# Summing the weight blocks of w_in elsewhere: from attention into slots and units

## The chip, the cores and the metric

The kernel runs on one core of a Trainium2 chip. The metric is the device time of one launch in microseconds, as the median of repeated runs. The core has five engines with queues of their own: TensorE (PE; its weight loads are shown apart as PEld), VectorE (DVE), ScalarE (ACT), GpSimd (POOL) and SyncE (SP), and sixteen DMA engines. GpSimd and SyncE issue most of the DMAs.

## The reference

Three parts follow each other, each fed by the one before:

```python
proj = einsum('bhsd,df->bhsf', x, w_phi)                 # attention, x = q and k
phi  = concat([exp(proj - max|proj|), exp(-(proj - max|proj|))])
kv, z = einsum('bhsf,bhsd->bhfd', k_p, v), sum(k_p, axis=2)
attn = einsum('bhsf,bhfd->bhsd', q_p, kv) / (q_p . z + 1e-6)

expert_idx = argmax(xn @ en.T / tau)                     # MoE, 8 experts, top 1
out[mask] = gate * (relu(x[mask] @ w1[e]) @ w2[e])

h = x @ w_in                                             # dense layer
out = (h * sigmoid(h)) @ w_out
```

Attention has 4 batches of 8 heads, 576 positions, head size 64 and 128 features. The MoE has 2304 tokens of 512 and experts of 1024. The dense layer goes 512 to 2048 to 512. All is fp32, except that w_in and w_out arrive as 64-bit floats.

## The kernel before

**Attention.** A loop `for g in range(-2, G)` runs over the 32 heads (G = 32). In each turn TensorE projects a head, multiplies phi(k) with v and phi(q) with kv, and works on neighbouring heads at the same time. VectorE's part of a head is always the same: the maximum (m, line 390), the difference (d, L391), the copy of kv (L470), the division (rd, lh and x, L486 to L491). GpSimd makes the low parts of fp32 operands (zl, L376; vl, L406; kl, L429). An fp32 matrix is split into a high part that TensorE multiplies at full rate and a low part that is what is left; a product is then three matmuls. Behind the last line of VectorE's work of a head stands, in chosen turns, other work: routing for the MoE (lines 557 to 617) and the preparation of w_in.

**Preparing w_in.** w_in is read as pairs of 32-bit integers and narrowed to fp32 on the chip by a chain of integer instructions (`narrow`, lines 179 to 205, one row of the profile for each step). Ten blocks of it, conversion step k = 0 to 9, are done in attention, in the turns listed in CONV, and more in the slots. The class `Convert` holds their buffers (raw). Two such blocks make a pair. The dense layer multiplies by Strassen-Winograd's scheme with seven products instead of eight, which needs four sums of the pair's four 256-column parts: `sums` makes them by three instructions, one over both of two parts (L174, 128x2x256) and two over one part (L177, 128x256). What comes out, seven columns of 256, is stored in DRAM (sscr, one for each of eight pairs) and fetched again later. Before the change pairs 2 to 6 are summed in attention by VectorE, two pairs by GpSimd in slots 11 and 16 (`csum`), and the last by VectorE in the third unit (`wsum`).

**Slots.** The MoE runs as 22 slots of 128 tokens (three more only run if the routing needs them). In a slot GpSimd gathers the tokens (xg), TensorE multiplies with w1 into ph and, after ScalarE's hh, with w2 into py. VectorE subtracts (xl, hl and the low part of the weights), ScalarE casts the high parts (wh, hh). Weights are loaded into buffers called raw. Between a slot's steps stand the remaining conversion of w_in and w_out and its loads and stores: STEPS gives (slot, step) of each VectorE and ScalarE piece, SLOTWORK those of loads (`cload`), sums (`csum`) and stores (`cstore`). Loads and stores in SLOTWORK are issued by GpSimd, in its own queue, in the order of the code, as are the gathers.

**Units.** The dense layer h = x @ w_in is 32 units: 8 pairs of column blocks for each of 4 groups of tokens, each of seven products (n) of about 0.8 us on TensorE, into puA, puB and puC, which ScalarE copies and VectorE joins (ht, L1120). In the first eight units each pair's weights are fetched from sscr (`wfetch`), copied to the high part (`whigh`, ScalarE) and reduced to the low part (`wlow`, VectorE, L1010, 128x1792). A list `at(u, n, task)` tells behind which product of which unit a task stands:

```python
for q in range(2, NJP):
    at(q - 2, 6, whigh, q)
    at(q - 1, 5, wlow, q)
at(1, 4, wfetch, 6)
at(2, 4, wfetch, 7)
at(3, 1, wsum)
```

The last layer multiplies with w_out and scatters to the output; the change doesn't touch it. All engines take their instructions in the order in which the code writes them; each waits for what its next instruction needs, and what stands behind it waits too.

Of the kernel before, what the change touches and what calls it, by code (L numbers as in the profile page):

```python
# [45 lines left out]
CT = 4  # L46
G = B * H
# [5 lines left out]
SUMS = 27  # L53
# [15 lines left out]
def moe_kernel(ctx, tc, qk, v, w_phi, emb, tau, w1, w2, win, wout, out):  # L69
# [11 lines left out]
    sscr = [dram.tile([P, 7 if i < NJP - 1 else 4, 256], F32, name=f"sscr{i}") for i in range(NJP)]  # L81
# [129 lines left out]
    class Convert:  # L211
# [3 lines left out]
        def region(self, p):  # L215
            return self.a[:, 2048:4096] if p == CA // 2 - 1 else self.b[:, p % 2 * 2048:(p % 2 + 1) * 2048]

        def load(self, i):
            o = (i + 1) % 3 * 1024
            self.h[i] = self.a[:, o:o + 1024].bitcast(I32).rearrange("p (f t) -> p f t", t=2)  # L220
            fetch_raw(i + CT, self.h[i])

        def step(self, k):
            if k + 2 < CA:
                self.load(k + 2)
            if k > 1:
                p = k // 2 - 1
                r = self.region(p).rearrange("p (a f) -> p a f", a=8)
                if k % 2 == 0:
                    self.s[p] = sums(r, nc.vector)  # L230
                    next(self.s[p])
                else:
                    next(self.s.pop(p), None)
            if k < CA:
                o = 512 * (k % 2 == 0)
                c = self.region(k // 2)[:, o:o + 512].bitcast(I32)
                todo = narrow(self.h.pop(k), c, k)
                next(todo)
# [12 lines left out]

    def phase_all(ctx):
# [725 lines left out]
        def wspace(q):  # L978
            if q == NJP - 1:
                W[q] = [wlast(0), None]  # L980
                return
            wb = (big.tile([P, 2, 2048], F32R, tag="blk", name="wb") if q < 4 else
                  pools["ur"].tile([P, 2, 7 * 256], F32R, tag=f"wb{q}", name="wbr", bufs=1))
            W[q] = wb[:, 0, 0:7 * 256], wb[:, 1, 0:7 * 256]

        def wlast(i, dt=F32R):
            return pools["ur"].tile([P, 7 * 256], dt, tag=f"wb{NJP - 1}{i}", name="wbr", bufs=1)

        def wfetch(q):
            if q < NJP - 1:  # L990
                if q not in W:
                    wspace(q)
                nc.sync.dma_start(out=W[q][1].bitcast(F32), in_=sscr[q].rearrange("p a f -> p (a f)"))
            else:
                W["r"] = pools["ul"].tile([P, 2048], F32, tag="ws", name="ws", bufs=2)
                nc.sync.dma_start(out=W["r"][:, 0:1024], in_=sscr[q].rearrange("p a f -> p (a f)"))

        def wsum():
            for _ in sums(W["r"].rearrange("p (a f) -> p a f", a=8), nc.vector):
                pass  # L1000

        def whigh(q):
            src = W[q][1].bitcast(F32) if q < NJP - 1 else W["r"][:, 256:]
            nc.scalar.copy(out=W[q][0], in_=src)

        def wlow(q):
            src = W[q][1].bitcast(F32) if q < NJP - 1 else W["r"][:, 256:]
            if q == NJP - 1:
                W[q][1] = wlast(1)
            nc.vector.tensor_tensor(out=W[q][1], in0=src, in1=W[q][0].bitcast(F32), op=ALU.subtract)  # L1010
# [207 lines left out]
        def rest():  # L1218
            xr = pools["ur"].tile([P, 2, TN], F32, tag="xf2", name="xf2", bufs=2)
            xr = xr.rearrange("p c t -> p (c t)")[:, 0:512]  # L1220
            rw, hs = FR[:, 0:512], FR[:, 512:1536]
            t1 = pools["ul"].tile([P, 2048], F32R, tag="ws", name="fr", bufs=2)
            ch_, cl_, xh_, xl_ = (t1[:, i * 512:(i + 1) * 512] for i in range(4))
# [64 lines left out]
        cv = Convert(*(raw2[i].rearrange("p k f -> p (k f)") for i in (1, 0)))  # L1288
        first = None
# [11 lines left out]
        for g in range(-2, G):  # L1301
# [231 lines left out]
        FR = wlast(1, F32)  # L1533
# [106 lines left out]
```

## Time and profile before

| | us |
|---|---|
| median of three runs (932.51 to 935.31) | 933.13 |
| profiled execution | 939.35 |
| its span in the trace | 937.6 |
| TensorE busy | 908.7 |
| VectorE busy | 643.5 |
| ScalarE busy | 583.0 |
| GpSimd busy | 238.5 |

The span begins with the first and ends with the last record of the profiled execution; the rest of its time lies around it. Attention reaches from the start to about 253 us (the first slot's products begin among its last heads, at 244.57 us), the slots follow, and then the units and the last layer, to the end. A busy time counts what an engine works on, not what it waits for; TensorE's matmuls overlap their weight loads. The granted clock of TensorE (PEclk) is given as a share of full speed; its mean in this execution is 0.989.

### The profile page before, as it was taken

The numbers are of one execution on the slowest core, as the hardware profiler recorded it, in microseconds if no ns is written. First come the engines' busy times: TensorE is split into PE (matmuls) and PEld (weight loads), VectorE is DVE, ScalarE is ACT, GpSimd is POOL, SyncE is SP. The second block draws the span as 40 slices with busy tenths as digits, with TensorE's granted clock in tenths as the row PEclk, the third lists the DMA queues.
The fourth block names the chain that finished last, engine by engine and source line by source line (L and its number), as shares of the span: only waits on it lengthen the run. The fifth ranks groups of instructions, "written<-read, shape, count | busy, mean of one in ns | idle before, by whom it ended". The sixth has DMA issues, their size and how long they took to land. (4 is left out here: it accounts for less than half of the span.)

```text
span 937.6 us, 15616 instructions
## 1 busy us (share of the span) xinstructions
PE 908.7 (97%) x5567; PEld 791.4 (84%) x5567; DVE 643.5 (69%) x982; ACT 583.0 (62%) x948; POOL 238.5 (25%) x221
## 2 busy tenths in 40 slices
PE   8999999998999999999999999999999999999996
PEld 6999999987767777887888789999999888888884
DVE  7899898997589989979998957675756222222220
ACT  6767878743686959969988765434456344443331
POOL 6887877821020320140400010101000110000000
PEclk9999999997999999999999999999999999999998
DMA  6354443338374671695298575777776844444410
GB/s 178 98 156 138 120 136 113 78 128 324 116 265 136 205 269 40 215 348 184 77 331 333 188 257 169 242 243 245 237 245 222 214 113 118 119 112 117 126 50 22
DMA packets 126898, 164.73 MB, mean 176 GB/s; under 512 B 34136, under 2 KB 88024, under 8 KB 126816
## 3 DMA queue, kind: packets, MB, share of 16 engines
q1 hardware_dynamic: 120704, 143.66, 48.6%
q0 software_dynamic: 6032, 19.99, 6.2%
q8 instruction: 45, 0.74, 0.3%
q14 instruction: 37, 0.30, 0.1%
q10 hardware_dynamic: 80, 0.03, 0.0%
HBM read 164.32 MB, written 45.48 MB: 224 GB/s over the span
## 5 line engine op out<-in xcount | busy, mean ns | idle before, releaser
L843 DVE TENSOR_TENSOR wl<-raw,wh 128x1024 fp32r<-128x1024 f32 (+1 forms) x166 | 190.4, 1192 | 29.0 <-ACT wh L842 21.6
L842 ACT CAST wh<-raw 128x1024 fp32r<-128x1024 f32 (+1 forms) x166 | 161.8, 1031 | 26.5 <-PE ph L795 13.5
L1190 DVE TENSOR_TENSOR hlt<-gt,hlt 128x1024 fp32r<-128x1024 f32 x34 | 41.7, 1226 | 146.4 <-ACT hlt L1189 146.4
L794 PE MATMUL po<-wob,hlt 128*128 128x512 f32 x272 | 108.5, 399 | 0.0
L1113 ACT COPY ht<-puA 128x288 f32<-128x288 f32 x128 | 51.0, 400 | 92.3 <-PE puA L795 86.6
L793 PE MATMUL po<-wob,hlt 128*128 128x512 f32 x272 | 107.2, 394 | 0.0
L795 PE MATMUL po<-wob,hlt 128*128 128x512 f32 x272 | 106.6, 392 | 0.0
L429 POOL TENSOR_TENSOR kl<-ke,kh 128x640 fp32r<-128x640 f32 x52 | 86.2, 1678 | 33.6 <-issue 27.2
L479 PE MATMUL pnx<-kv,qp 128*128 128x73 f32 x640 | 78.7, 279 | 0.0
L1210 ACT COPY os<-po 128x512 f32<-128x512 f32 x17 | 10.0, 588 | 108.3 <-PE po L795 108.3
L479 PEld LDWEIGHTS pnx<-kv,qp 128*128 128x128 f32 x640 | 76.2, 196 | 0.1
L795 PE MATMUL ph<-wh,xl 128*128 128x512 f32 x166 | 65.3, 394 | 1.8 <-DVE xl L850 1.8
L793 PE MATMUL ph<-wh,xh 128*128 128x512 f32 x166 | 67.0, 404 | 0.0
L794 PE MATMUL ph<-wl,xh 128*128 128x512 f32 x166 | 64.8, 390 | 0.0
L414 ACT ACTIVATE ke<-d 128x640 f32<-128x640 f32 x52 | 38.3, 737 | 41.4 <-DVE d L391 41.4
L1211 POOL DMA_INDIRECT out<-os,oidx x18 | 17.6, 976 | 179.1 <-ACT os L1210 168.6
L384 PE MATMUL pqk<-wbd,zh 128*128 128x256 f32 (+1 forms) x320 | 61.0, 290 | 1.7 <-DVE d L391 1.5
L793 PEld LDWEIGHTS po<-wob,hlt 128*128 128x128 f32 x272 | 51.1, 188 | 13.1
L1120 DVE TENSOR_TENSOR ht<-puC,ht 128x288 f32<-128x288 f32 x64 | 29.0, 453 | 48.0 <-PE puC L795 41.3
L795 PEld LDWEIGHTS po<-wob,hlt 128*128 128x128 f32 x272 | 51.1, 188 | 12.3
L794 PEld LDWEIGHTS po<-wob,hlt 128*128 128x128 f32 x272 | 51.0, 188 | 11.8
L1022 POOL DMA_INDIRECT yt<-yd,yidx x13 | 14.1, 1081 | 166.9 <-PE pt L1039 77.9
(407 smaller groups left out, 2472.6 us busy)
## 6 DMA issues: line engine op xcount, KB each, us to landing
raw<-w SPq DMA_DIRECT2D x44, 1536.0 KB
raw<-w SPq DMA_DIRECT2D x44, 512.0 KB
hd<-ht SPq DMA_DIRECT2D x124, 144.0 KB
gt<-hd SPq DMA_DIRECT2D x15, 1024.0 KB
z<-qk SPq DMA_DIRECT2D x32, 288.0 KB
wo<-wout SPq DMA_DIRECT2D x16, 512.0 KB
yd<-ys SPq DMA_DIRECT2D x23, 256.0 KB
raw<-win SPq DMA_DIRECT2D x10, 512.0 KB
```

The lines of the kernel that those rows point to most:

```text
L384: nc.tensor.matmul(out=pqk[0:r, c * 256:(c + 1) * 256], lhsT=z[:, c * P:c * P + r], rhs=wbd[:, j].rearrange("p h f -> p (h f)"), start=(i ...
L414: nc.scalar.activation(out=ke, in_=kd, func=AF.Exp, scale=1.0 - 2.0 * s)
L429: nc.gpsimd.tensor_tensor(out=kl[:, :, s, :], in0=st.pop(("ke", g, s)), in1=kh[:, :, s, :].bitcast(F32), op=ALU.subtract)
L479: nc.tensor.matmul(out=pn[:, c, 0:73], lhsT=qp[:, s, c * P:(c + 1) * P], rhs=kv[:, s, 0:73], start=(s == 0), stop=(s == 1))
L793: nc.tensor.matmul(out=o, lhsT=ah, rhs=bh, start=first, stop=False, skip_group_check=more)
L794: nc.tensor.matmul(out=o, lhsT=ah, rhs=bl, start=False, stop=False, skip_group_check=more)
L795: nc.tensor.matmul(out=o, lhsT=al, rhs=bh, start=False, stop=last, skip_group_check=more)
L842: nc.scalar.copy(out=hi[:, 0:n], in_=sl[:, 0:n])
L843: nc.vector.tensor_tensor(out=lo[:, 0:n], in0=sl[:, 0:n], in1=hi[:, 0:n].bitcast(F32), op=ALU.subtract)
L1113: nc.scalar.copy(out=htile(u, at), in_=BK[u, "A"])
L1120: nc.vector.tensor_tensor(out=o, in0=BK[u, b], in1=o, op=ALU.add)
L1190: nc.vector.tensor_tensor(out=lo, in0=g, in1=hi.bitcast(F32), op=ALU.subtract)
```

## The change

Of the five pairs that attention sums, it now sums two, 2 and 3, in the turns of SUMS (3, 5, 6 and 12, 19, 20). Pairs 4 to 7 are stored as plain columns (`keep_weights`, four columns of 256) and summed by VectorE in units 2 to 5; `wsum` takes the pair's number, stands behind the first product, `whigh` behind the second, and `wlow` behind the first of the unit after. The two sums by GpSimd stay in slots 11 and 16. The four conversion steps of J1 that stood in slots 4 and 5 stand in slots 7 and 8. Of the loads of w_in that stood next to each other in slot 7, one is now in slot 4 and one in slot 8. The store of pair 0's half in slot 6 becomes two stores of plain columns, in slots 3 and 8. The tiles of the last four pairs' weights are cut in two (`wside`); the work on overflow (`rest`), which doesn't run here, uses other buffers.

```diff
-SUMS = 27
+SUMS = {3: 0, 5: 0, 6: 0, 12: 1, 19: 1, 20: 1}
...
+    def keep_weights(i, c, dma=nc.sync):
+        q, odd = divmod(i, 2)
+        o = 2 * (1 - odd)
+        dma.dma_start(out=sscr[q][:, o:o + 2, :], in_=c.bitcast(F32).rearrange("p (a f) -> p a f", a=2))
...
         def step(self, k):
+            if k > 4:
+                keep_weights(k - 1 + CT, self.done(k - 1))
             if k + 2 < CA:
                 self.load(k + 2)
-            if k > 1:
-                p = k // 2 - 1
-                r = self.region(p).rearrange("p (a f) -> p a f", a=8)
-                if k % 2 == 0:
-                    self.s[p] = sums(r, nc.vector)
-                    next(self.s[p])
-                else:
-                    next(self.s.pop(p), None)
...
+                yield from narrow(self.h.pop(k), self.done(k), k)
+
+        def pair(self, p):
+            r = self.b[:, p * 2048:(p + 1) * 2048].rearrange("p (a f) -> p a f", a=8)
+            yield from sums(r, nc.vector)
+            yield
+            nc.sync.dma_start(out=sscr[CT // 2 + p], in_=r[:, 1:8])
...
+        def cplain(i):
+            keep_weights(i + NJ - 2, J[i][0][:, 0:512], nc.gpsimd)
+
-        SLOTWORK = {(6, 1): (cstore, 0), (7, 1): (cload, 2), (7, 3): (cload, 3),
+        SLOTWORK = {(3, 1): (cplain, 0), (4, 1): (cload, 2), (8, 3): (cplain, 1), (8, 7): (cload, 3),
                     (11, 1): (csum, 1), (13, 1): (cstore, 1), (13, 5): (cload, 4), (13, 7): (cload, 5),
                     (16, 1): (csum, 2), (16, 3): (cstore, 2)}
-        STEPS = [(2, 1), (2, 3), (2, 5), (2, 7), (4, 1), (4, 5), (5, 1), (5, 5)]
+        STEPS = [(2, 1), (2, 3), (2, 5), (2, 7), (7, 1), (7, 5), (7, 7), (8, 1)]
...
+            if g in SUMS:
+                next(pairs[SUMS[g]], None)
             if g in BITS:
                 nv(2)
-            if g == SUMS:
-                nv(9)
...
-            for q in range(2, NJP):
+            for q in (2, 3):
                 at(q - 2, 6, whigh, q)
-                at(q - 1, 5, wlow, q)
-            at(1, 4, wfetch, 6)
-            at(2, 4, wfetch, 7)
-            at(3, 1, wsum)
+                at(q - 1, 5 if q == 2 else 1, wlow, q)
+            for q in range(4, NJP):
+                at(q - 2, 1, wsum, q)
+                at(q - 2, 2, whigh, q)
+                at(q - 1, 1, wlow, q)
+            at(3, 5, wfetch, 6)
+            at(4, 5, wfetch, 7)
```

VectorE near the end of attention, turn g = 26: lh and x are the last of a head, the rows from tb on are routing, raw is a block of w_in. Before:

```order
L489 TENSOR_TENSOR lh<-pnx,rd 128x40
L491 TENSOR_TENSOR x<-pnx,rd 128x5x64
L174 TENSOR_TENSOR raw_1_159<-raw_1_159 128x2x256
L177 TENSOR_TENSOR raw_1_159<-raw_1_159 128x256 x2
L606 TENSOR_TENSOR tb_2868<-oh,vec 128x120 x2
L608 TENSOR_REDUCE al_2869<-tb_2868 128x30
```

After:

```order
L482 TENSOR_TENSOR lh<-pnx,rd 128x40
L484 TENSOR_TENSOR x<-pnx,rd 128x5x64
L599 TENSOR_TENSOR tb_2862<-oh,vec 128x120 x2
L601 TENSOR_REDUCE al_2863<-tb_2862 128x30
L602 TENSOR_TENSOR al_2863<-al_2863,rq 128x15
```

The three sums of the last pair that attention made are gone, and routing stands right behind the head.

GpSimd from the first slots on: xg are the gathers of tokens, x<-win the loads of w_in, sscr<-x the stores, ag a piece of routing. Before:

```order
L828 DMA xg<-xd,gidx 128x512 x3
L171 DMA x<-win 128x4x256 x2
L828 DMA xg<-xd,gidx 128x512 x5
L731 TENSOR_TENSOR ag<-am_3577,gp 128x20x25 x3
L828 DMA xg<-xd,gidx 128x512
L949 DMA sscr_74<-x 128x512 x2
L828 DMA xg<-xd,gidx 128x512
L171 DMA x<-win 128x4x256 x2
L828 DMA xg<-xd,gidx 128x512 x4
```

After:

```order
L821 DMA xg<-xd,gidx 128x512 x3
L172 DMA x<-win 128x4x256 x2
L821 DMA xg<-xd,gidx 128x512 x3
L177 DMA sscr_74<-x 128x512
L821 DMA xg<-xd,gidx 128x512
L172 DMA x<-win 128x4x256
L821 DMA xg<-xd,gidx 128x512
L724 TENSOR_TENSOR ag<-am_3571,gp 128x20x25 x3
L821 DMA xg<-xd,gidx 128x512 x3
L177 DMA sscr_74<-x 128x512
L172 DMA x<-win 128x4x256
L821 DMA xg<-xd,gidx 128x512 x3
```

The two loads that stood together stand five gathers apart, with a store ahead of each.

VectorE in the units where the weights of pairs 4 to 7 are made: ht are the joins of products, ws the plain columns, wbr the low part of a pair. Before:

```order
L1120 TENSOR_TENSOR ht<-puC,ht 128x288
L174 TENSOR_TENSOR ws<-ws 128x2x256
L177 TENSOR_TENSOR ws<-ws 128x256 x2
L1010 TENSOR_TENSOR wbr<-wbr 128x1792
L1120 TENSOR_TENSOR ht<-puC,ht 128x288
L1120 TENSOR_TENSOR ht<-puB,ht 128x288
L1120 TENSOR_TENSOR ht<-puC,ht 128x288
L1010 TENSOR_TENSOR wbr<-wbr 128x1792
```

After:

```order
L1117 TENSOR_TENSOR ht<-puC,ht 128x288
L1007 TENSOR_TENSOR wbr<-ws,wbr 128x1792
L180 TENSOR_TENSOR ws<-ws 128x2x256
L183 TENSOR_TENSOR ws<-ws 128x256 x2
L1117 TENSOR_TENSOR ht<-puC,ht 128x288
L1117 TENSOR_TENSOR ht<-puB,ht 128x288
L1117 TENSOR_TENSOR ht<-puC,ht 128x288
L1007 TENSOR_TENSOR wbr<-ws,wbr 128x1792
```

The low part stands ahead of the sums instead of behind them, and the sums come in four units instead of one.

## Rows read from the trace of the kernel before

**Rows 1.** The page's first part: busy us, share of the span, instructions.

```profile
PE 908.7 (97%) x5567; PEld 791.4 (84%) x5567; DVE 643.5 (69%) x982; ACT 583.0 (62%) x948; POOL 238.5 (25%) x221
```

**Rows 2.** Waits of TensorE: line, what it waits for, us in total, times, longest.

```profile
PE pnx L623 <- DVE x L491: 3.4, 1, 3.4
...
PE py L793 <- ACT hh L847: 2.1, 1, 2.1
PE ph L795 <- DVE xl L850: 1.8, 3, 1.0
...
PE puA L795 <- DVE wbr L1010: 0.7, 1, 0.7
```

**Rows 3.** Timeline, TensorE, attention's end: start, us, instruction, [idle before, releaser].

```profile
213.43 0.48 PE L384 MATMUL pqk<-wbd,zh 128*128 128x256 f32 x2 [0.61 <-DVE d L391]
...
218.46 2.32 PE L445 MATMUL pkv<-kl,ve 128*65 128x256 f32 x10
...
224.16 0.42 PE L623 MATMUL pnx<-at,bm 128*128 128x12 bf16 x10 [3.38 <-DVE x L491]
...
225.05 0.78 PE L384 MATMUL pqk<-wbd,zh 128*128 128x256 f32 x2
...
234.49 3.94 PE L445 MATMUL pkv<-kl,ve 128*65 128x256 f32 x10
```

**Rows 4.** Windows: from:to, us, busy PE PEld DVE ACT POOL, PEclk, DMA share, GB/s.

```profile
228.00:230.00 2.00, 2.00 (x11) 2.00 (x10) 1.37 (x1) 0.00 (x0) 1.27 (x2) 0.50 0.92 266
340.00:345.00 5.00, 5.00 (x25) 4.06 (x23) 4.27 (x11) 0.00 (x0) 0.00 (x0) 1.00 1.03 371
345.00:350.00 5.00, 2.79 (x12) 1.88 (x11) 2.53 (x4) 3.89 (x7) 0.99 (x1) 1.00 0.55 193
```

**Rows 5.** Instructions of L174 and L177: ns least/median/most, first and last start.

```profile
L174 DVE TENSOR_TENSOR raw<-raw x5: 681/681/685, 49.1 to 214.3; 128x512 f32<-128x512 f32 x5
...
L177 DVE TENSOR_TENSOR raw<-raw x10: 414/424/427, 62.6 to 215.5; 128x256 f32<-128x256 f32 x10
```

**Rows 6.** Timeline of VectorE and GpSimd at g = 1, 12 and 14.

```profile
35.62 0.42 DVE L188 TENSOR_SCALAR raw<-raw 128x512 f32<-128x512 f32 x1
...
112.38 3.33 POOL L429 TENSOR_TENSOR kl<-ke,kh 128x640 fp32r<-128x640 f32 x2 [1.00 <-POOL vl L406]
...
112.50 1.80 DVE L188 TENSOR_SCALAR raw<-raw 128x512 f32<-128x512 f32 x1
...
126.72 0.68 DVE L174 TENSOR_TENSOR raw<-raw 128x512 f32<-128x512 f32 x1
127.32 0.42 DVE L188 TENSOR_SCALAR raw<-raw 128x512 f32<-128x512 f32 x1
```

**Rows 7.** Timeline of TensorE: the projections around g = 12.

```profile
112.31 0.40 PE L384 MATMUL pqk<-wbd,zh 128*128 128x256 f32 x2
...
119.07 0.47 PE L384 MATMUL pqk<-wbd,zh 128*128 128x256 f32 x2
...
126.49 0.40 PE L384 MATMUL pqk<-wbd,zh 128*128 128x256 f32 x2
```

**Rows 8.** Windows over VectorE's steps of g = 23 and g = 26.

```profile
185.22:193.90 8.68, 8.68 (x80) 8.68 (x79) 8.30 (x21) 4.26 (x8) 4.26 (x3) 1.00 0.46 168
210.28:219.95 9.67, 9.06 (x65) 7.49 (x64) 9.29 (x21) 3.89 (x8) 1.41 (x1) 1.00 0.84 317
```

**Rows 9.** Timeline of VectorE in slot 4: the conversion's step.

```profile
315.15 0.68 DVE L203 SCALAR_TENSOR_TENSOR x<-x 128x512 int32<-128x512 int32 x1
```

**Rows 10.** Timeline of GpSimd and ScalarE in slot 7: a load, and the wait for w2.

```profile
333.87 0.77 POOL L171 DMA_DIRECT2D x<-win  x1 [0.31 <-DMA sscr<-x]
...
346.11 0.62 ACT L842 CAST wh<-raw 128x512 fp32r<-128x512 f32 x1 [8.19 <-DMA raw<-w]
```

**Rows 11.** Timeline of VectorE in the third and fourth units.

```profile
559.61 0.69 DVE L174 TENSOR_TENSOR ws<-ws 128x512 f32<-128x512 f32 x1 [2.93 <-DMA ws<-sscr]
...
561.14 2.02 DVE L1010 TENSOR_TENSOR wbr<-wbr 128x1792 fp32r<-128x1792 f32 x1
```

More of the change, by code (lines that the diff above doesn't have):

```diff
@@ L46 @@
 CT = 4
+QD = 4
 G = B * H
@@ L80, in moe_kernel @@
     yd = dram.tile([NT + 2 * P, DM], F32, name="yd")
-    sscr = [dram.tile([P, 7 if i < NJP - 1 else 4, 256], F32, name=f"sscr{i}") for i in range(NJP)]
+    sscr = [dram.tile([P, 7 if i < QD else 4, 256], F32, name=f"sscr{i}") for i in range(NJP)]
     woscr = [dram.tile([P, 2, DM], F32, name=f"woscr{i}") for i in range(NJP)]
@@ L213, in __init__, with done @@
             self.a, self.b, self.h, self.s = a, b, {}, {}
-        def region(self, p):
-            return self.a[:, 2048:4096] if p == CA // 2 - 1 else self.b[:, p % 2 * 2048:(p % 2 + 1) * 2048]
+        def done(self, i):
+            p, even = divmod(i, 2)
+            o = 512 * (1 - even)
+            return (self.b[:, p * 2048 + o:p * 2048 + o + 512] if p < 2 else self.a[:, 3072 + o:3584 + o]).bitcast(I32)
         def load(self, i):
-            o = (i + 1) % 3 * 1024
+            o = i % 3 * 1024
             self.h[i] = self.a[:, o:o + 1024].bitcast(I32).rearrange("p (f t) -> p f t", t=2)
@@ L978, in wspace @@
         def wspace(q):
[L979 to L987, printed above, removed]
+            if q < 4:
+                wb = big.tile([P, 2, 2048], F32R, tag="blk", name="wb")
+                W[q] = [wb[:, 0, 0:7 * 256], wb[:, 1, 0:7 * 256]]
+            else:
+                W[q] = [wside(q, i) if q < NJP - 2 or q + i < NJP - 1 else None for i in range(2)]
@@ L989, in wfetch, with wside @@
+        def wside(q, i, dt=F32R):
+            return pools["ur"].tile([P, 7 * 256], dt, tag=f"wb{q}{i}", name="wbr", bufs=1)
         def wfetch(q):
-            if q < NJP - 1:
-                if q not in W:
-                    wspace(q)
+            if q < QD:
+                wspace(q)
                 nc.sync.dma_start(out=W[q][1].bitcast(F32), in_=sscr[q].rearrange("p a f -> p (a f)"))
             else:
-                W["r"] = pools["ul"].tile([P, 2048], F32, tag="ws", name="ws", bufs=2)
-                nc.sync.dma_start(out=W["r"][:, 0:1024], in_=sscr[q].rearrange("p a f -> p (a f)"))
@@ L998, in wsum, with wsource @@
-        def wsum():
-            for _ in sums(W["r"].rearrange("p (a f) -> p a f", a=8), nc.vector):
-                pass
+                W["r", q] = pools["ul"].tile([P, 2048], F32, tag="ws", name="ws", bufs=2)
+                nc.sync.dma_start(out=W["r", q][:, 0:1024], in_=sscr[q].rearrange("p a f -> p (a f)"))
+        def wsum(q):
+            for _ in sums(W["r", q].rearrange("p (a f) -> p a f", a=8), nc.vector):
+                pass
+        def wsource(q):
+            return W["r", q][:, 256:] if q >= QD else W[q][1].bitcast(F32)
@@ L1002, in whigh, with wtile @@
+        def wtile(q, i):
+            if W[q][i] is None:
+                W[q][i] = wside(q, i)
+            return W[q][i]
         def whigh(q):
-            src = W[q][1].bitcast(F32) if q < NJP - 1 else W["r"][:, 256:]
-            nc.scalar.copy(out=W[q][0], in_=src)
+            nc.scalar.copy(out=wtile(q, 0), in_=wsource(q))
         def wlow(q):
-            src = W[q][1].bitcast(F32) if q < NJP - 1 else W["r"][:, 256:]
-            if q == NJP - 1:
-                W[q][1] = wlast(1)
@@ L1010, in wlow @@
-            nc.vector.tensor_tensor(out=W[q][1], in0=src, in1=W[q][0].bitcast(F32), op=ALU.subtract)
+            nc.vector.tensor_tensor(out=wtile(q, 1), in0=wsource(q), in1=W[q][0].bitcast(F32), op=ALU.subtract)
         def tiles_of(k):
@@ L1220, in rest @@
             xr = xr.rearrange("p c t -> p (c t)")[:, 0:512]
-            rw, hs = FR[:, 0:512], FR[:, 512:1536]
-            t1 = pools["ul"].tile([P, 2048], F32R, tag="ws", name="fr", bufs=2)
-            ch_, cl_, xh_, xl_ = (t1[:, i * 512:(i + 1) * 512] for i in range(4))
+            rw, hs = FR[2][:, 0:512], FR[2][:, 512:1536]
+            ch_, cl_, xh_, xl_ = FR[1][:, 0:512], FR[1][:, 512:1024], FR[0][:, 0:512], FR[0][:, 512:1024]
             for s in range(NSF, NS):
@@ L1288, in phase_all @@
         cv = Convert(*(raw2[i].rearrange("p k f -> p (k f)") for i in (1, 0)))
+        pairs = [cv.pair(p) for p in range(2)]
         first = None
@@ L1392, in phase_all @@
                 cg[0] = cv.step(CONV.index(g))
+                if g == CONV[-1]:
+                    nv(9)
             if g in (G - H + 1, G - H + 3):
@@ L1532, in phase_all @@
             wspace(q)
-        FR = wlast(1, F32)
+        FR = wside(NJP - 2, 1), wside(NJP - 1, 0), wside(NJP - 1, 1, F32)
         wfetch(4)
```

19 lines of the change are left out of this document (1 added, 18 removed).

## The prediction, made before the changed kernel was run

> **What bounds the kernel now.** I read the page's first part, then TensorE's waits over the whole span, then each place that they name, and there the order of work on the engine that was late. TensorE is busy for 97% of 937.6 us [rows 1], so only its pauses are for sale. It has few [rows 2]: 3.4 us for VectorE's x at the end of attention, 2.1 us for ScalarE's hh in a slot, 1.8 us in three waits for xl, 0.7 us for wbr in the first units. Two losses don't show there: matmuls that are dealt out a little late behind a slow VectorE, and matmuls that run at half the clock. Both are found below.
>
> **The clock.** At the end of attention TensorE ends ten matmuls of 2.32 us at 220.78 and next starts at 224.16, idle for 3.38 us [rows 3]; from there the granted clock is 0.50, that is 1.2 and not 2.4 GHz [rows 4], and the same ten matmuls of the next head take 3.94 us [rows 3]. From the projection ahead of the first ten to their end it is 7.35 us (213.43 to 220.78), at half clock 13.37 us (225.05 to 238.42), so the fall costs 13.4 - 7.4 = 6.0 us. In slot 7 an idle of 2.11 us [rows 2] left the clock at 1.00 [rows 4]. So between 2.1 and 3.4 us of idle lies what brings the fall here. The profiled execution took 939.35 us, its span 937.6; the median of the timed runs is 933.13. Without the fall the profiled one would be 939.35 - 6.0 = 933.3, the median within 0.03%. I take it that the timed runs mostly don't have the fall, and make the sum against 933.3 and then the median. Against the profiled execution itself the fall would be one more term, -6.0.
>
> **The change part by part.** A pair's sums on VectorE are one instruction of 0.68 and two of 0.42 us, and all ten plus five of them in attention are of that length [rows 5]. Three of five pairs leave attention, 3 x (0.68 + 2 x 0.42) = 4.6 us of VectorE, spread over g = 7, 12, 14, 21, 23 and 26. What each is worth depends on whether VectorE is late there.
>
> (a) g = 12. Two sums go, one first sum comes. Before, VectorE does the two and then a conversion instruction at 112.50, just after GpSimd has begun on kl (112.38), and it takes 1.80 us; two steps later the conversion behind the single first sum (126.72) starts at 127.32 and takes 0.42 us [rows 6]. TensorE pays for the long one: from the projection at 119.07 to that at 126.49 are 7.42 us, after 6.76 for the one before [rows 7]. After the change g = 12 has the order of g = 14, so I take -0.7 (7.42 - 6.76), between 0 and -0.8. At g = 7, 14 and 21 the first sum goes and the conversion starts 0.7 us sooner; at g = 1, which never had a sum, the conversion took 0.42 us [rows 6], so nothing is lost there, and nothing gained where TensorE isn't late.
> The Trainium skill (SBUF — State Buffer, "Who interferes with whom") says that VectorE and GpSimd share a pair of ports as an exclusive lock, and that whichever starts first keeps it for its whole instruction. The two lengths, 0.42 and 1.80 us, agree. By that rule a sum taken out can also move a conversion into the lock; with g = 7, 14 and 21 hit as g = 12 was, the sum would be 3 x 0.7 = 2.1 us worse, and the row of g = 1 speaks against it.
>
> (b) g = 23. Two sums of 0.42 go from a step of 8.68 us in which VectorE is busy for 8.30 [rows 8]. Worth 0 to -0.84; I take -0.8, as VectorE is what is full there.
>
> (c) g = 26. All three go, 1.5 us (0.68 + 2 x 0.42 [rows 5]), from a step of 9.67 us with VectorE busy 9.29 [rows 8]. Everything after them on VectorE, as far as the x for which TensorE idles 3.38 us, comes that much earlier, and the idle becomes about 1.9 us. Late next is the same x. -1.5, between 0 and -1.5.
>
> (d) Slots 4 to 6. VectorE loses two instructions of 0.68 (the first is at 315.15 [rows 9]) and one of 0.42, ScalarE one. VectorE works without a pause from the first of them to the xl for which TensorE waits ([rows 2], 1.0 us the longest), so that xl is 0.7 us earlier: -0.7, between 0 and -1.0. The instruction of 0.42 stands ahead of a place where VectorE waits for ScalarE, and is worth nothing.
>
> (e) Slot 7. GpSimd's queue started two loads of win one right after the other, the second at 333.87 [rows 10]; from 340 to 345 the DMA engines are full (1.03, 371 GB/s [rows 4]), and ScalarE stands 8.19 us for w2 until 346.11 [rows 10], with hh behind it, for which TensorE idles 2.11 us. After the change one load is issued in slot 4, the other at the end of slot 8. A megabyte less at 371 GB/s is 2.8 us; w2 then lands about 343.3 (346.1 - 2.8), and what hangs on it is more than TensorE's 2.11 us earlier. I take -2.0, between 0 and -2.1.
>
> (f) Slots 7 and 8 gain the three VectorE instructions that slots 5 and 6 lose: 0.42 + 2 x 0.68 = 1.8 us. From 340 to 345 VectorE is busy for 4.27 of 5 us [rows 4], so there is little room, but its parts of the weights are made ahead of their matmuls; +0.3, between 0 and +1.8. The moved loads: slot 4's comes behind a gather that waits for routing, and the next conversion of it is in slot 9; slot 8's waits for a store in GpSimd's queue and is used in slot 10. Gathers behind them are two slots early. No cost taken.
>
> (g) Units. Before, pair 7's sums wait 2.93 us for their data in unit 3, and wlow for pair 4 stands behind them (561.14, 2.02 us) [rows 11], while TensorE waits 0.7 us for it [rows 2]. Now wlow stands ahead of the sums. TensorE loses no more there: -0.8, between 0 and -1.0. The four sets of sums (4 x 1.5 us) lie on an engine that waits for TensorE's products most of the time there, at worst beside the joins; ScalarE's whigh moves to just ahead of a copy of puA that TensorE needs two products later, which would cost some tenths per unit: 0 to +1.0, taken as 0. The six stores of single columns in attention carry less than the three of sums that go.
>
> Sum: -0.7 - 0.8 - 1.5 - 0.7 - 2.0 + 0.3 - 0.8 = -6.2. 933.13 - 6.2 = 926.9 us. Bounds: 0.8 + 0.8 + 1.5 + 1.0 + 2.1 + 1.0 = 7.2 below, 1.8 + 1.0 above if every gain fails.
>
> **The rivals.**
> *The clock falls in the timed runs too, and no longer after.* For it: the idle of 3.38 us is in every run, and the change cuts it to 1.9, under the 2.11 that left the clock alone. Against it: 939.35 - 6.0 meets the median. Time 926.9 - 6.0 = 920.9.
> The Trainium skill (TensorE: Matmul & The Clock Gate, "What's actually happening") says that the gate looks at the engine's activity on a schedule that does not start with the kernel, so that one idle may bring a fall in one run and not in another. No run here shows the timed runs' clock. By this rule the median before could stand with some falls in it; that is this rival.
> *Half of it.* Where VectorE was late it is late again, at the next wait: in (a) and (b) time given back in attention is taken by the routing steps that follow, and in (d) to (f) slots 7 and 8 spend what 5 and 6 saved. Then only (c) and (e) stay: 933.13 - 3.5 = 929.6.
> *Nothing arrives.* The gains of VectorE are met by ScalarE or DMA, which were as late: 933 within 1.5.
> *Slower.* In slot 7 w2 stays late for another reason (its buffer, not the traffic), TensorE's 2.11 us stay, and the 1.8 us that VectorE now has there come on top: 3.9 us of idle, over the 3.38 that brought the fall. Place slot 7, price 1.8 + 6.0 = 7.8, decided by whether that idle passes 3.4 us. With (a) to (d) and (g) at -4.5: 933.13 - 4.5 + 7.8 = 936.4. Against it: the full DMA engines at 340 to 345.
>
> **How the numbers follow.** Forecast 926.9: 0.48. Clock 920.9: 0.24. Half 929.6: 0.12. Nothing: 0.10. Slower 936.4: 0.06. 0.3% (about what a measurement here can tell from no change) is 2.8 us, so faster means under 930.3. Faster: 0.45 + 0.24 + 0.08 = 0.77. Same: 0.03 + 0.04 + 0.10 = 0.17. Slower 0.06. The range takes the clock rival with a microsecond and a half below it (919.4) and reaches up to 932.0, where "half" is in and most of "nothing" and all of "slower" are left out.
>
> **What would show it.** In the profile after: the conversion at g = 12 at 0.42 us; TensorE's wait for x near 1.9 us and the granted clock 1.00 behind it; no wait of ScalarE for w2 of microseconds in slot 7; the wait for xl under 0.5 us; none for wbr in the units. Wrong if the clock falls anywhere between attention and the end, if VectorE in slots 7 and 8 becomes what TensorE waits for, or if the sums in units 4 and 5 wait for their data and copies of puA behind them make TensorE wait.

## The result and the profile after

The changed kernel took 925.06 us in the median of four runs (923.90 to 926.33), the kernel before 934.14 us beside it (932.51 to 935.31): 9.1 us less, a ratio of 0.9904 with a 95% interval of 0.9881 to 0.9927. The forecast was 926.9, that is 6.2 us less than 933.13. The profiled execution took 924.59 us where that of before took 939.35, 14.8 us less, of which 6.0 are the fall of the clock that the prediction had kept out of its sum.

TensorE's waits over the span, after (line, releaser, us in total, times, longest), answer to [rows 2]:

```profile
PE puA L786 <- ACT ht L1110: 1.6, 3, 0.8
PE py L786 <- ACT hh L840: 1.6, 1, 1.6
...
PE ph L788 <- DVE xl L843: 1.2, 3, 0.4
...
PE pnx L616 <- DVE x L484: 0.7, 1, 0.7
...
PE puC L786 <- DVE ht L1117: 0.6, 1, 0.6
```

The wait for x fell from 3.4 us to 0.7, the longest for xl from 1.0 to 0.4, and the one for wbr is gone. The wait for hh seems to have stayed, with 1.6 in place of 2.1 us, but it isn't the same one: it has moved from slot 7 to slot 13. Of the 1.6 us for puA, 1.3 stood there before.

One wait of attention is neither in [rows 2] nor in this list. TensorE waits for kvt, which ScalarE copies behind work that VectorE holds up (d, for the most part); before and after:

```profile
PE pkv L467 <- ACT kvt L460: 3.3, 7, 0.9
...
PE pkv L460 <- ACT kvt L453: 1.2, 3, 0.5
```

The waits that are gone stood, among others, at 93.58, 121.46, 149.43 and 199.99, which are the places where TensorE gains behind g = 7, 12, 14 and 23 in the table below. So VectorE's lateness at these places did show among TensorE's waits, as the second largest of them.

Both programs give TensorE the same 5567 matmuls in the same order, so the start of one and the same matmul can be compared in the two traces. This table is read from TensorE's timelines, for the first matmul that is shown at each place:

| place | before | after | gained so far |
|---|---|---|---|
| attention, products with kv, two heads after g = 7 | 96.09 | 95.27 | 0.8 |
| attention, behind g = 12 | 126.03 | 124.42 | 1.6 |
| attention, behind g = 14 | 150.05 | 147.60 | 2.4 |
| attention, behind g = 23 | 204.14 | 199.76 | 4.4 |
| the matmul that waits for x | 224.16 | 217.15 | 7.0 |
| end of the stretch at half clock | 240.05 | 227.00 | 13.0 |
| slot 7, ahead of its w2 | 330.02 | 316.36 | 13.7 |
| slot 7, behind its w2 | 348.11 | 331.79 | 16.3 |
| slot 12 | 378.17 | 361.68 | 16.5 |
| slot 13, behind its w2 | 426.20 | 411.14 | 15.1 |
| fifth unit | 564.12 | 548.11 | 16.0 |
| ninth unit | 588.00 | 572.97 | 15.0 |
| seventeenth unit | 636.02 | 621.26 | 14.8 |

So, in the traces, attention gave 7.0 us, the clock 6.0, slots 4 to 12 3.5, and slot 13 took 1.4 back; the units gave 1.0 and took 1.3 back, of which 0.6 are a wait that other executions of the changed kernel don't have (below). Without the clock it is 8.8.

### The profile page after: what moved, and what is told of

It is laid out like the page before. It is cut to its first block, busy times and chain, and to the rows that moved or that the text cites. A ratio compares the mean times of both kernels' runs of the same rounds, so it can differ in the third digit from the quotient of the medians.

```text
span 922.9 us, 15620 instructions
## 1 busy us (share of the span) xinstructions
PE 900.4 (98%) x5567; PEld 785.7 (85%) x5567; DVE 636.8 (69%) x982; ACT 582.3 (63%) x948; POOL 243.0 (26%) x221
## 5 line engine op out<-in xcount | busy, mean ns | idle before, releaser
L1110 ACT COPY ht<-puA 128x288 f32<-128x288 f32 x128 | 50.8, 400 | 88.8 <-PE puA L788 76.7
L472 PE MATMUL pnx<-kv,qp 128*128 128x73 f32 x640 | 76.6, 275 | 0.0
L472 PEld LDWEIGHTS pnx<-kv,qp 128*128 128x128 f32 x640 | 74.1, 192 | 0.1
```

The lines of the kernel that those rows point to most:

```text
L472: nc.tensor.matmul(out=pn[:, c, 0:73], lhsT=qp[:, s, c * P:(c + 1) * P], rhs=kv[:, s, 0:73], start=(s == 0), stop=(s == 1))
L1110: nc.scalar.copy(out=htile(u, at), in_=BK[u, "A"])
```

## The experiments

**The removed sums put back.** To the changed kernel, with pair p's block r:

```diff
+        def again(g):
+            p = int(g < 20)
+            r = cv.b[:, p * 2048:(p + 1) * 2048].rearrange("p (a f) -> p a f", a=8)
+            if g in (7, 14, 21, 26):
+                next(sums(r, nc.vector))
+            if g in (23, 26):
+                for o in (5, 6):
+                    nc.vector.tensor_tensor(out=r[:, o], in0=r[:, o - 1], in1=r[:, o - 3], op=ALU.add)
...
+            if g != 26:
+                again(g)
...
+                again(g)
```

> The changed kernel with the removed sums put back on VectorE in attention, as repetitions of sums on blocks that attention has summed or will sum: one over two parts at g = 7, 14 and 21, two over one part at g = 23, all three at g = 26. Slots and units stay as changed. Theory A (a sum costs what its removal pushes out of GpSimd's way): attention loses what the trace of after had gained there: 0.8 at g = 7, 0.8 at g = 14, 0 at g = 21, 1.9 at g = 23, 2.6 at g = 26 = 6.1 us, so 925.1 + 6.1 = 931.2, with the conversion at g = 7 back at 1.8 us, and a TensorE idle of about 3.3 us for x. Rival B (my own sum): 0 + 0 + 0 + 0.8 + 1.5 = 2.3 us, 927.4. If the idle of 3.3 us brings the fall of the clock in every run, 6.0 us more: 937 by A.

Measured: 932.65 us in the median of 12 runs (930.30 to 938.75). Matmul by matmul against the changed kernel's trace, stretches at half clock left out, it loses 0.8 us after g = 7, 0.2 after g = 14, nothing after g = 21, 1.9 after g = 23 and 2.65 at g = 26: 5.6 us, near theory A's 6.1 and far from B's 2.3. What misses is g = 14: its sum costs 0.2 when g = 12 has the new order, and 0.8 went with it in the change. The rest of that 0.8 then belongs to g = 12, whose lateness VectorE had carried along; no run shows that by itself. The time between runs varies by 8 us, and so does the clock; that is taken up below.

**One sum less at two places of the kernel before.**

```diff
-    def sums(r, eng):
+    def sums(r, eng, n=2):
...
-        for o in (5, 6):
+        for o in (5, 6)[:n]:
...
-                    self.s[p] = sums(r, nc.vector)
+                    self.s[p] = sums(r, nc.vector, 2 if p < 3 else 1)
...
+            if g == 1:
+                nc.vector.memset(cv.a[:, 3584:3840], 0.0)
```

> The kernel before without one of the two sums of 0.42 us at g = 23 and one at g = 26 (column 6 of pairs 5 and 6 isn't computed; a fill of 256 columns on VectorE at g = 1, where it has time, stands for one of them). Nothing else changes. Theory A: the two routing instructions that take 1.33 us at g = 23 and 1.29 us at g = 26 start 0.4 us earlier, ahead of GpSimd's zl, and take 0.2: each place gives 0.42 + 1.1 = 1.5 us, together -3.0: 931.1, TensorE's idle for x from 3.4 to about 1.9. Rival B (a queue with fixed lengths): -0.42 each, -0.8: 933.3, the routing instructions still 1.3 us.

Measured: 936.25 us (12 runs, 932.53 to 942.46) against 936.40 for the kernel before, ratio 0.9985 (0.9958 to 1.0012). The times don't decide: the interval holds the ratios of both A (0.997) and B (0.999). The trace does. TensorE gains 0.5 us at g = 23 and 0.4 at g = 26, which is B's number, but not because lengths are fixed. VectorE (DVE) and GpSimd (POOL) at g = 23 and g = 26, in the kernel before:

```profile
191.49 0.20 DVE L502 TENSOR_TENSOR lt<-lg,mx 128x40 f32<-128x40 f32 x1
191.72 1.33 DVE L505 TENSOR_TENSOR lt<-lt,em 128x40 f32<-128x40 f32 x1
...
191.60 1.40 POOL L376 TENSOR_TENSOR zl<-z,zh 128x576 fp32r<-128x576 f32 x1 [3.52 <-ACT zh L370]
...
216.80 1.29 DVE L609 TENSOR_TENSOR al<-al,rq 128x15 f32<-128x15 f32 x1
...
216.66 1.41 POOL L376 TENSOR_TENSOR zl<-z,zh 128x576 fp32r<-128x576 f32 x1 [7.24 <-ACT zh L370]
```

with one sum less:

```profile
191.64 0.20 DVE L505 TENSOR_TENSOR lt<-lt,em 128x40 f32<-128x40 f32 x1
...
192.11 1.32 DVE L509 TENSOR_TENSOR oh<-em8c,mx 128x40 bf16<-128x40 f32 x1
...
191.97 1.40 POOL L376 TENSOR_TENSOR zl<-z,zh 128x576 fp32r<-128x576 f32 x1 [3.53 <-ACT zh L370]
...
216.25 0.17 DVE L609 TENSOR_TENSOR al<-al,rq 128x15 f32<-128x15 f32 x1
...
216.67 1.33 DVE L611 SCALAR_TENSOR_TENSOR al<-al 128x15 f32<-128x15 f32 x1
```

and in the changed kernel:

```profile
187.61 0.20 DVE L498 TENSOR_TENSOR lt<-lt,em 128x40 f32<-128x40 f32 x1
...
188.57 0.16 DVE L510 TENSOR_TENSOR ohs<-ohs 128x8 bf16<-128x8 bf16 x1
...
188.88 1.40 POOL L369 TENSOR_TENSOR zl<-z,zh 128x576 fp32r<-128x576 f32 x1 [4.14 <-ACT zh L363]
...
210.91 0.17 DVE L602 TENSOR_TENSOR al<-al,rq 128x15 f32<-128x15 f32 x1
...
212.21 0.82 DVE L557 TENSOR_TENSOR bm<-jot,lo 128x640 bf16<-128x640 f32 x1
...
212.28 2.00 POOL L369 TENSOR_TENSOR zl<-z,zh 128x576 fp32r<-128x576 f32 x1 [7.24 <-ACT zh L363]
```

A routing instruction of 15 or 40 elements a partition takes 0.17 or 0.20 us, or 1.3 us if it starts just after GpSimd's zl, and then ends when zl does. With one sum less, the instruction that was hit (L505, L609) goes free and one behind it (L509, L611) is hit in its place. Only if all of them are through before zl starts is the 1.1 us saved, as in the changed kernel, where VectorE comes to g = 23 with less arrears and has 0.84 us less to do there. At these two places the gain comes in a step: the first 0.42 us give 0.4 to 0.5, what then brings the last instruction past zl gives 1.1 more.

**The slots alone.** The kernel before with the slots' part:

```diff
-        SLOTWORK = {(6, 1): (cstore, 0), (7, 1): (cload, 2), (7, 3): (cload, 3),
+        SLOTWORK = {(3, 1): (cplain, 0), (4, 1): (cload, 2), (8, 3): (cplain, 1), (8, 7): (cload, 3),
...
-        STEPS = [(2, 1), (2, 3), (2, 5), (2, 7), (4, 1), (4, 5), (5, 1), (5, 5)]
+        STEPS = [(2, 1), (2, 3), (2, 5), (2, 7), (7, 1), (7, 5), (7, 7), (8, 1)]
```

> The kernel before with the slots' part of the change alone: J1's four steps in slots 7 and 8, one load of w_in in slot 4 and one in slot 8, the two stores of plain columns in slots 3 and 8. Attention and units as before. By the trace of after: slots 4 to 6 -0.6, slot 7 and 8 -2.2, slot 13 +1.4 (its w2 then comes too late): -1.4, 932.7. My prediction's steps (d) to (f): -2.4, 931.7, and no new wait in slot 13. A rival in which slot 13's loss came from the earlier end of attention: -2.8, 931.3, no wait in slot 13.

Measured: 934.82 us (12 runs, 932.72 to 938.42), ratio 0.9972 (0.9948 to 0.9997), 1.6 us between the medians. In the trace, the clock left out, the gain is 0.6 us ahead of slot 7, 2.8 there, and at slot 13 1.8 are lost again, 1.6 in all, with attention as before:

```profile
417.17 0.50 PE L793 MATMUL py<-wh,hh 128*128 128x512 f32 x1 [1.95 <-ACT hh L847]
```

So the wait for hh in slot 13 comes from the slots' own part, and the rival by which it came from attention is out. What the moved loads and what the moved conversion steps give isn't separated here.

**A load out of slot 13.** The changed kernel with

```diff
-                    (11, 1): (csum, 1), (13, 1): (cstore, 1), (13, 5): (cload, 4), (13, 7): (cload, 5),
+                    (11, 1): (csum, 1), (13, 1): (cstore, 1), (13, 5): (cload, 4), (14, 1): (cload, 5),
```

> The changed kernel with the second of slot 13's two loads of w_in (512 KB) issued in slot 14, behind a gather. If these loads take DMA time ahead of w2 in slot 13 (512 KB at 390 GB/s are 1.3 us), TensorE's idle of 1.57 us for hh there falls to 0.2 or so: 925.1 - 1.3 = 923.8. If w2 is late for another reason (its buffer): the idle stays and the time is 925.1. If the load then comes too late for slot 15: a wait of VectorE for it there, and up to +2 us.

Measured: 923.71 us (6 runs, 922.57 to 924.17). That is where the changed kernel itself came out on another chip (923.30, below), so the times don't decide. In the trace TensorE's wait for hh is 0.7 us and not 1.6, half of what was expected: GpSimd reached the load at 402.14, only 2.2 us later than in the changed kernel (399.94), since its queue runs ahead of the slots. Why slot 13 waits, in the changed kernel, is seen in the windows (us, busy PE, PEld, DVE, ACT, POOL, PEclk, DMA share, GB/s), ScalarE's and TensorE's timelines:

```profile
395.00:405.00 10.00, 10.00 (x48) 8.02 (x47) 6.61 (x7) 3.99 (x5) 3.11 (x3) 1.00 1.04 401
```

```profile
397.11 3.89 ACT L835 CAST wh<-raw 128x1024 fp32r<-128x1024 f32 x4 [2.01 <-DMA raw<-w]
407.20 0.62 ACT L835 CAST wh<-raw 128x512 fp32r<-128x512 f32 x1 [6.19 <-DMA raw<-w]
...
408.36 0.50 PE L786 MATMUL py<-wh,hh 128*128 128x512 f32 x1 [1.57 <-ACT hh L840]
```

The DMA engines are full there, with the slot's weights, four stores of a summed pair and two loads of w_in. In the kernel before the same stretch was as full (1.01 from 405 to 415), and TensorE did not wait for hh there. What has changed is where TensorE is when the four stores are issued (before, after):

```profile
404.01 2.22 POOL L949 DMA_DIRECT2D sscr<-x  x4
...
388.72 2.23 POOL L941 DMA_DIRECT2D sscr<-x  x4
```

The stores come 15.3 us earlier, TensorE at slot 12 is 16.5 us earlier. This difference, 1.2 us, is near the 1.4 that slot 13 loses; no run tests it alone. Not every gain is lost in a full stretch: the 7.0 us of attention passed it, and so does most of what the sums cut in two gain (below).

**whigh later.** The changed kernel with

```diff
-                at(q - 2, 2, whigh, q)
+                at(q - 2, 4, whigh, q)
```

> The changed kernel with ScalarE's whigh of pairs 4 to 7 behind the fourth product of a unit and not the second. If whigh, waiting for the sums with copies of puA queued behind it, is what made TensorE late by 0.5 us at the start of the seventh unit (561.5), that goes: -0.5, or -0.8 with the two later waits for VectorE's ht if these hang on it. If another copy of puA is hit in its place: 0.

Measured: 930.45 us (6 runs, 929.29 to 931.69), 7 us slower than the changed kernel on the same chip (923.30): neither 0 nor a gain. ScalarE's whigh and TensorE, with whigh behind the fourth product:

```profile
540.96 1.69 ACT L1004 CAST wbr<-ws 128x1792 fp32r<-128x1792 f32 x1 [1.15 <-DVE ws L183]
548.52 1.69 ACT L1004 CAST wbr<-ws 128x1792 fp32r<-128x1792 f32 x1 [1.20 <-DVE ws L183]
...
543.00 0.40 PE L786 MATMUL puA<-xcT,wb 128*128 128x288 f32 x1 [1.22 <-ACT ht L1110]
550.56 0.40 PE L786 MATMUL puA<-xcT,wb 128*128 128x288 f32 x1 [0.84 <-ACT ht L1110]
```

Behind the fourth product, copies of puA stand close after whigh, which waits for the sums, and each of four units loses 0.6 to 1.4 us, 4.4 in all; 1.0 of it is made up in the next units by waits that only the changed kernel has. The profiled execution lost about 3.4 us more to two stretches of 3.4 us at half clock, one behind a wait of 1.71 us for hh in slot 13 (from 409.5), one behind the third of these losses (from 559.7). Behind the second product, only the whigh of the sixth unit costs a wait, of 0.33 us (561.50, [0.33 <-ACT ht L1110]). The place that the change chose is the better one.

**Sums in g = 10 and 18.** The changed kernel with

```diff
-SUMS = {3: 0, 5: 0, 6: 0, 12: 1, 19: 1, 20: 1}
+SUMS = {10: (0, 0), 11: (0,), 18: (1, 1), 19: (1,)}
...
-            if g in SUMS:
-                next(pairs[SUMS[g]], None)
+            for p in SUMS.get(g, ()):
+                next(pairs[p], None)
```

> The changed kernel with the sums of pairs 2 and 3 moved into g = 10 and g = 18 as a whole (there VectorE was busy for 4.74 of 6.6 us), out of g = 3, 5, 12 and 19. The step at g = 5 and that at g = 19 take 8.27 us each, with conversions of 1.80 and 1.77 us behind the two sums. Theory A: without sums these conversions run ahead of GpSimd's kl and take 0.42, the steps fall to 6.7, and TensorE gains what it pays there, 0.86 (6.84 + 7.44 - 2 x 6.71) and 0.70 (7.40 - 6.70): -1.5 us. Rival: the sums meet kl at g = 10 and 18, are blocked there or block it, and give back up to 0.7 us each: 0 to -0.2.

Measured: 926.45 us (6 runs, 924.39 to 930.23), slower than the changed kernel. Both theories were right in a part: the step at g = 5 fell to 6.6 us and that at g = 19 to 7.3, and TensorE got 0.9 and 0.7 back, but at g = 10 and 18 the sums met kl,

```profile
96.67 0.75 DVE L180 TENSOR_TENSOR raw<-raw 128x512 f32<-128x512 f32 x1
97.46 2.25 DVE L183 TENSOR_TENSOR raw<-raw 128x256 f32<-128x256 f32 x2
...
97.40 1.57 POOL L422 TENSOR_TENSOR kl<-ke,kh 128x640 fp32r<-128x640 f32 x1 [0.52 <-POOL vl L399]
```

two sums that take 0.84 took 2.25, and each place cost 1.4 us: 1.1 us lost at the end of attention. The profiled execution also waited 4.3 us for hh in slot 13 and ran at half clock after it.

**The clock.** Two kernels: the changed one unaltered, and the changed one with the three sums at g = 26 put back (the edit of the first experiment, with 26 alone).

> The changed kernel itself, unaltered, on the same chip as the other three, for the spread of its times and mean clocks against those of the kernel before. If TensorE's idle of 3.4 us for x is what lowers the clock for a varying stretch, the changed kernel, which idles there for 0.7 us, has mean clocks of 0.995 or more and times between 922 and 927 in nearly all runs, where the kernel before spreads from 932 to 943. If other causes lower the clock, it spreads as widely.

> The changed kernel with three sums put back at g = 26 alone (repetitions, on blocks that are stored already). VectorE's step there goes from 7.0 to 9.7 us and TensorE's idle for x from 0.7 to about 3.3. Theory: that idle alone brings the fall of the clock; the fastest runs are 2.6 us slower than those of the changed kernel (about 926), the median some 2 to 4 us more on top, mean clocks spread down to 0.987. Rival (the clock of the kernel before has another cause, or needs the other sums too): every run 2.6 us slower, with mean clocks of 0.995 or more.

Measured: 923.30 us for the changed kernel (5 runs, 922.84 to 924.09, mean clock 0.997 in each), 928.56 with the sums at g = 26 (8 runs, 927.59 to 933.54, mean clocks from 0.990 to 0.996), 935.69 for the kernel before beside them (13 runs, 933.65 to 941.28). TensorE at the wait for x, and the window behind it, with the sums at g = 26:

```profile
219.85 0.39 PE L616 MATMUL pnx<-at,bm 128*128 128x12 bf16 x10 [3.37 <-DVE x L484]
```

```profile
220.00:230.00 10.00, 9.20 (x70) 8.02 (x67) 4.99 (x11) 3.89 (x10) 3.07 (x3) 0.83 0.64 226
```

and in the changed kernel:

```profile
217.15 0.39 PE L616 MATMUL pnx<-at,bm 128*128 128x12 bf16 x10 [0.74 <-DVE x L484]
```

```profile
220.00:230.00 10.00, 9.54 (x76) 8.31 (x75) 5.57 (x10) 5.00 (x10) 1.95 (x3) 1.00 0.95 331
```

The idle of 3.4 us is back with the sums, and the fall of the clock with it, for a shorter stretch than in [rows 4]. Even the fastest run is 4.7 us slower than the fastest of the changed kernel, 2.6 by the idle itself (3.37 - 0.74). So the idle brings a fall, and its length differs from run to run: in the traces with this idle the clock is at half for 13.7 us behind 3.38 us (the kernel before, and all sums back), for 3.4 us behind 3.39 (slots alone) and 3.37 (sums at g = 26), and for 10.2 us behind 2.97 (one sum less); no trace with the short idle has a fall there. Over the 51 runs of the kernel before that stood beside the experiments, the time goes from 932.63 to 943.19 us and the mean clock from 0.996 to 0.986, by 0.9 us for each 0.001 (the fall of [rows 4] gives nearly the same price: 6.0 us for 13.7 us at half clock, which are 0.0073 of the mean); of 14 runs of the changed kernel none is under 0.995. A line for each kernel measured, through its points of time and mean clock, with one slope for all, puts the kernel before at 933.4 and the changed one at 925.0 where the clock is 0.996: 8.5 us, near the 8.8 of the traces without the fall. What is left of the 12 to 13 us between the medians on one chip goes with the clock. (A mean under 1 isn't a fall by itself: with TensorE done, each trace ends with 6 to 9 us at half clock.)

**Sums cut in two, and slot 13.** Three kernels beside the changed one on the same chip: attention's two-sum steps cut in two, the stores and the load of slot 13 moved, and both.

```diff
-SUMS = {3: 0, 5: 0, 6: 0, 12: 1, 19: 1, 20: 1}
+SUMS = {3: 0, 5: 0, 6: 0, 7: 0, 12: 1, 13: 1, 19: 1, 20: 1}
...
         for o in (5, 6):
+            if o == 6:
+                yield
...
-                    (11, 1): (csum, 1), (13, 1): (cstore, 1), (13, 5): (cload, 4), (13, 7): (cload, 5),
+                    (11, 1): (csum, 1), (11, 3): (cstore, 1), (13, 5): (cload, 4), (15, 0): (cload, 5),
```

> The changed kernel with the second step of each pair's sums in attention cut in two: one sum of 0.42 at g = 5 and one at g = 6, one at g = 13 and one at g = 19, where two stood together at g = 5 and g = 19. Theory A (what counts is how many instructions start behind kl): with one sum ahead only the second conversion instruction of g = 5 and g = 19 is held up and not both, these steps fall from 8.27 to about 6.7 us as at g = 3, and TensorE gets back 0.86 at g = 5 and 0.70 at g = 19; the sums at g = 6 and 13 cost VectorE 0.4 each in steps whose second instruction waits for kl in any case: -1.1 to -1.5. Rival (the sums' own time counts, 0.42 saved in each place and 0.42 spent in another): 0.

> The changed kernel with less DMA traffic ahead of slot 13's w2: the four stores of a summed pair (896 KB) right behind GpSimd's sums in slot 11, where the DMA engines have time (0.66 busy from 385 to 390), and not in slot 13, and the second load of w_in in slot 15. If the queue of transfers in slot 13 is what TensorE waits for (1.3 to 1.6 us), the wait goes: -1.3 in a typical run, and no run in which it brings the clock down. Rival (w2 waits for its buffer): the wait stays, 0.

> The changed kernel with the sums cut in two and slot 13's stores and load moved. If the gains of attention and of slot 13 add up: -2.4 to -2.8 against the changed kernel on the same chip. If what attention gains is lost at the next full stretch of the DMA engines, as in slot 13 of the changed kernel: -1.3 or less.

> The changed kernel itself once more, on the chip of the three others, to compare them with: 923 to 925.

Measured: the changed kernel 924.74 us (5 runs, 922.83 to 926.12), sums cut in two 923.12 (4 runs, 921.84 to 925.04), slot 13 923.31 (4 runs, 922.36 to 924.70), both 921.36 (5 runs, 920.88 to 922.16). The ratios to the kernel before on that chip are 0.9860 (0.9838 to 0.9882), 0.9854 (0.9830 to 0.9878), 0.9854 (0.9831 to 0.9877) and 0.9829 (0.9810 to 0.9848). Each half alone is within the spread of the changed kernel, with both every run is below every one of its runs. In the traces cutting the sums gains 1.8 us in attention, more than was expected, since at g = 5 neither of the conversion's instructions is held up any more,

```profile
62.50 0.41 DVE L185 TENSOR_TENSOR raw<-raw 128x256 f32<-128x256 f32 x1
62.83 0.42 DVE L196 TENSOR_SCALAR raw<-raw 128x512 f32<-128x512 f32 x1
63.17 0.42 DVE L192 TENSOR_SCALAR raw<-raw 128x512 int32<-128x512 int32 x1
...
63.16 3.35 POOL L424 TENSOR_TENSOR kl<-ke,kh 128x640 fp32r<-128x640 f32 x2 [1.04 <-issue]
```

and with the stores and the load moved slot 13's wait falls from 1.20 to 0.15 us:

```profile
407.01 0.50 PE L786 MATMUL py<-wh,hh 128*128 128x512 f32 x1 [0.15 <-ACT hh L840]
```

With the sums cut in two alone, 1.5 of the 1.8 us are still there behind slot 13, although its DMA is as full as before; with both, 1.6 us come from attention, and 2.4 are there behind slot 13. So the two gains add up, and the rival by which slot 13 takes what attention gains is out. This is the fastest version measured.

## Why the prediction was right, and where its steps weren't

The time came out 1.8 us under the forecast, inside the range, and the reason given for most of it (VectorE late in attention, the wait for x, the full DMA in slot 7) is what the runs show. But the sum's parts didn't measure what they were given: without the clock they come to 8.8 us in the traces, where the sum had 6.2. That the time was met so closely is partly luck. The median that the forecast started from (933.13, three runs) is among the fast ones of the kernel before, whose later 51 runs have a median of 936.67; against the runs beside it the changed kernel is 12.4 us (923.30 to 935.69) and 13.1 us (924.74 to 937.81) faster, twice the 6.2.

- **(a), g = 12.** The long conversion went as forecast: the projections of [rows 7] are now 6.71 and 6.70 us apart, for 6.76 and 7.42. The step "nothing gained where TensorE isn't late" failed: TensorE was late behind g = 7 and 14 as well, and the waits for kvt (above) showed it. At g = 7 the removed sum let the conversion's second instruction start ahead of kl (VectorE and GpSimd, after):

```profile
77.68 0.42 DVE L194 TENSOR_SCALAR raw<-raw 128x512 f32<-128x512 f32 x1
78.01 0.42 DVE L187 TENSOR_SCALAR raw<-raw 128x512 int32<-128x512 int32 x1
...
78.34 1.56 POOL L422 TENSOR_TENSOR kl<-ke,kh 128x640 fp32r<-128x640 f32 x1 [1.02 <-issue]
```

  It had taken 1.79 us (78.56, kl at 78.28), and VectorE was late in the routing steps right behind, where TensorE got 0.8 back. Another 0.8 came behind g = 14, by the first experiment (0.2 for its own sum) mostly as g = 12's arrears. Only g = 21 gave TensorE nothing at once; it took arrears of VectorE away ahead of g = 23, where its step now starts 3.3 us earlier (185.22 to 181.90) and TensorE stands 2.4 us earlier.
- **(b), g = 23**, forecast -0.8, measured -1.9; **(c), g = 26**, forecast -1.5, measured -2.6. Both terms counted the sums' own length. What they left out is the routing instruction of 1.3 us at each place, which the prediction took as given. The two steps now (windows, answering to [rows 8]) are 1.9 and 2.6 us shorter:

```profile
181.90:188.65 6.75, 6.75 (x62) 6.75 (x61) 6.41 (x18) 4.20 (x8) 2.84 (x2) 1.00 0.61 191
205.91:212.94 7.03, 6.42 (x48) 5.37 (x47) 6.72 (x18) 3.89 (x8) 0.66 (x1) 1.00 0.73 278
```

- **VectorE beside GpSimd.** The rule of the Trainium skill (SBUF — State Buffer, "Who interferes with whom") had been weighed as a risk only, that a sum less could move a conversion into the lock. By the same rule a sum less moves instructions out of it, and at all six places an instruction that had taken 1.3 to 1.8 us takes 0.17 to 0.42. The runs agree with the rule that who starts first holds the other off, in both directions: VectorE's 0.17 against 1.3 us behind zl and 0.84 against 2.25 behind kl, GpSimd's zl 1.40 against 2.00 us behind VectorE's bm.
- **(d)** -0.7, measured -0.6. **(e)** -2.0, measured -2.7 in slot 7: the wait for w2 is gone as worked out, and the gain is over the 2.11 us that bounded it, since the first matmuls behind the wait had come late too (0.85 us from 347.26 to 348.11, now 0.54). **(f)** +0.3, measured -0.2 over slots 8 to 12. What was missing is a term for slot 13, +1.4: the prediction asked what is late next in the slot that it mended and not at the next full stretch of DMA, where the stores had not come forward as far as TensorE.
- **(g)** -0.8. The wait for wbr went, -1.0. The cost of whigh, bounded by 0 and +1.0 and taken as 0, was 0.5 at the start of the seventh unit, and VectorE's joins took 0.3 more. A further 0.6 at the sixteenth unit isn't the change's: two other executions of the changed kernel lost 0.7 and 0.9 us less at that place than the one shown.
- **The clock.** The step "the timed runs mostly don't have the fall" failed. It rested on one equation, 939.35 - 6.0 = 933.3, which the median of three runs met. By the mean clocks the kernel before falls in most runs, for stretches of different length, and its median over 51 runs is 936.67. The rival "the clock falls in the timed runs too" was true, and its 920.9 was missed because it took the whole 6.0 us from a median that held little of it. The inference that a fall needs an idle between 2.1 and 3.4 us fell as well (below).

## What to carry to other kernels

What an instruction costs on VectorE, where GpSimd works beside it, is read from what it pushes behind GpSimd's start: look at each small instruction that takes several times its usual length, and ask which edit brings all of them ahead of it. A gain of TensorE that the DMAs don't gain with it can be lost at the next full stretch of DMA, so after each wait that goes, look for the next place where the DMA engines are full, and for what sets the start of their transfers, not only for the next wait. Read the whole list of waits before a place is called free: here the second largest was left out. And when TensorE's clock falls in the profiled execution, look at clock and time of many runs before the fall is kept out of a sum.

## What the runs showed of the hardware

An idle of TensorE of 2.11 us in slot 7 had left the clock at full speed in the kernel before. With the sums put back, an idle of 1.96 us in slot 13 was followed by a fall, and one of 1.71 us in slot 13 with whigh later, while one of 1.95 us in slot 13 with the slots alone left the clock alone. Windows over slot 13 with the slots alone, and behind it with whigh later (columns as above):

```profile
410.00:420.00 10.00, 7.94 (x37) 6.05 (x36) 3.81 (x6) 3.98 (x7) 2.02 (x2) 1.00 1.04 391
...
410.00:420.00 10.00, 10.00 (x41) 7.84 (x41) 9.03 (x9) 10.00 (x16) 0.00 (x0) 0.86 0.55 204
```

Two pauses of 0.58 and 0.94 us near 196 and 198 were followed by a fall, too, with the sums put back, where the kernel before has nearly the same two pauses (0.57 and 0.93) and kept its clock. Windows of the kernel with the sums put back:

```profile
196.00:198.00 2.00, 1.60 (x14) 1.34 (x12) 1.97 (x5) 0.92 (x2) 0.00 (x0) 1.00 0.12 27
198.00:200.00 2.00, 1.46 (x13) 1.46 (x14) 1.83 (x7) 1.88 (x4) 0.00 (x0) 1.00 0.63 156
200.00:202.00 2.00, 2.00 (x14) 2.00 (x14) 1.97 (x3) 0.75 (x3) 1.41 (x1) 0.63 0.32 122
202.00:204.00 2.00, 2.00 (x9) 1.61 (x9) 1.14 (x6) 1.36 (x2) 0.00 (x0) 0.51 0.00 0
```

So a pause of the same length is followed by a fall in one execution and not in another. This agrees with the Trainium skill (TensorE: Matmul & The Clock Gate, "What's actually happening"), by which the gate's schedule doesn't start with the kernel; what of the pauses decides in one run stays open here. Also unexpected was how small an instruction can be held up for nearly the whole of a GpSimd instruction: 15 elements a partition, 0.17 us alone, 1.3 us behind GpSimd's zl of 1.4.
